# Windowed attention and a softplus feed-forward on one core: the holds on the first loads, and the order of the opening

## The chip, the cores and the metric

One core of one Trainium2 chip runs the whole program. The metric is the device time of one launch in microseconds (us); the runs of the kernel before had a median of 815.86 us (three runs, 813.49 to 820.68).

## The reference

```python
def _attn_ref(q, k, v):                    # 8 batches, 8 heads, 576 positions, 64 wide
    scores = scale * np.matmul(q, k.transpose(0, 1, 3, 2))
    mask_plain = (rel >= 0) & (rel < window)                                # window 32
    mask_dil = (rel >= 0) & (rel < window * dilation) & (rel % dilation == 0)   # dilation 4
    ...
    scores = np.where(masks[None, :, :, :], scores, -1000000000.0)
    attn = np.exp(scores - np.max(scores, axis=-1, keepdims=True))
    attn = attn / (np.sum(attn, axis=-1, keepdims=True) + 1e-09)
    return np.matmul(attn, v).astype(np.float32)

def _moe_ref(x, w_in, w_out):              # 4608 tokens, 512 wide, 2048 inside
    h = x @ w_in
    g = np.maximum(h, 0.0) + np.log1p(np.exp(-np.abs(h)))
    return (g @ w_out).astype(np.float32)
```

Half of the heads see the last 32 positions, half see 32 positions four apart. The result of the attention goes through a feed-forward layer with softplus between its two matrices. Inputs are float32; the two matrices come to the chip as 64-bit words.

## The kernel before

The 4608 tokens are nine chunks of 512. Four groups of two heads (two plain, two dilated) make a chunk's attention; their results, turned, are the chunk's x, and 16 slices of 128 columns of the inner layer follow. Each float32 operand of the large products is split into a high and a low part, so that a product is three matmuls. Later chunks go through a planner; both kernels share it and everything it makes.

The opening is not planned. It covers the first two chunks and the decoding of the first matrices, and its order is a string of words, OPENING (line 93). A loop behind the functions (from line 794 on) runs the words one by one. Each engine, and SP's queue of DMAs too, keeps the order in which the words issue its instructions. The words, with a group g, a chunk or a slice behind the letters:

- k, q, v, m, r: loads of a group's keys, queries and values, of a chunk's mask, and of a 128x512 piece of a matrix in 64-bit words (`raw`, two halves). All go to SP's queue except k0, k1 (line 758, on ACT's queue) and m0 (ACT's too).
- S: the scores of a group on TensorE, tile `s_ps`. For the first two chunks the mask is added by two more matmuls. M: the maximum (DVE, lines 410 and 415). E: eight exponentials (ACT, line 433). Z and P or Pv: sums, reciprocal, division (DVE, lines 445 to 453). T: four transposes on TensorE, tile `t_ps`. C or Cv: copying them out. V: the weighted values, tile `a_ps`. Xh, Xl: the high and low part of x.
- D0 to D5 and Dl: the seven steps that turn one `raw` piece into a matrix's high and low part, tile `parts`. D0 and D5 stand on ACT (lines 205 and 228), the others on DVE (207 to 231).
- H, A, G, Gs or Gh, Gl, O: the first product, softplus on ACT and DVE, its two parts `gh` and `gl` (line 704), the second product.
- F with a number: so many matmuls on a block of zeros that nobody reads, tile `unread` ("fillers").
- A word with @ behind it: its first load is held back until the last matmul of the word named there.

Besides the hold, `load_dma` (line 163) keeps at most eight of SP's first loads under way, and a load into a buffer waits for the last reader of what stood there. Queries of the first chunk have buffers of their own; q4, q5 and q6 use three in turn, and q7 takes that of q4. Every load raises one of eight semaphores, DMAHW0 to DMAHW7, taken in turn in the order in which the scheduler places the loads, and waits until the load that had that semaphore before it has landed.

```python
    def load_dma(engine=None, **kw):
        ins = tc.keep_in_program_order((engine or nc.sync).dma_start(**kw))
        if held[0] is not None:
            tc.add_manual_dep(
                ins.ins,
                held[0].ins.name,
    ...
    for word in OPENING.split():
        word, _, awaited = word.partition("@")
        held[0] = last_of.get(awaited)
    ...
        parts[name](*(int(x) for x in word[len(name) :].split("_")))
        last_of[word] = last_matmul[0]
```

Of the kernel before, what the change touches and what calls it, by code (L numbers as in the profile page):

```python
# [90 lines left out]


OPENING = """
k0 F1 m0 k1 q0 q1@F1 S0 M0 S1 E0 F6 r0 M1 Z0 r1 k2@S0 F1 q2 Pv0 D0_0_0 D0_1_0 E1 D1_0_0 q3 D1_1_0 S2 D2_0_0
D2_1_0 D3_0_0 v0 T0 M2 Z1 k3@S0 S3 m1@F6 r2@S1 C0 D3_1_0 Pv1 V0 D4_0_0 k4@S2 q4@F1 v1@F1 E2 D0_0_1 M3 k5@S3
D4_1_0 T1 Xh0 D5_0_0 S4 Cv1 r3@F1 q5@F1 D1_0_1 Z2 D2_0_1 Xl0 M4 E3 v2@F6 F3 Pv2 E4 V1 Xh1 Z3 T2 D0_2_0 Dl0_0
D3_0_1 Pv3 H0_0 Cv2 v3@V1 D5_1_0 S5 r4@S3 Xl1 D4_0_1 M5 T3 D1_2_0 C3 Dl1_0 r5 D5_0_1 V2 D2_2_0 Xh2 H0_1 E5 v4@T3
Xl2 Z4 H1_0 Pv4 Dl0_1 V3 Xh3 D3_2_0 Xl3 D4_2_0 D0_3_0 r6 D1_3_0 D2_3_0 T4 H0_2 C4 Z5 r7@H0_1 H0_3 H1_1 D0_1_1
D1_1_1 D5_2_0 A0 V4 v5@T4 D3_3_0 Xh4 Dl2_0 G0 H1_2 q7@H1_1 H1_3 Xl4 D0_4_0 Pv5 Gs0 H2_0 A1 r8@H0_2 D4_3_0 Gl0
H2_1 H2_2 k7@H0_3 T5 D1_4_0 D5_3_0 D2_1_1 H2_3 G1 k6@H2_2 O0_0 C5 Dl3_0 V5 D3_1_1 D2_4_0 O0_1 Gs1 Xh5 D0_2_1 r9  # L100
D4_1_1 O0_3 H3_0 H3_1 Gl1 Xl5 D1_2_1 D5_1_1 A2 D3_4_0 D2_2_1 Dl1_1 D4_4_0 S7 O0_2 G2 D0_5_0 H3_2 O1_1 M7 O1_2
D5_4_0 Dl4_0 H3_3 D3_2_1 r10 H4_0 Gs2 D1_5_0 r11 q6@O0_2 O1_3 E7 D4_2_1 v7@O0_2 D5_2_1 A3 H4_1 H4_2 Gl2 v6
D2_5_0 D0_3_1 D3_5_0 Dl2_1 D4_5_0 S6 M6 H4_3 D5_5_0 O2_1 O2_3 O2_2 O1_0 E6 D0_4_1 G3 Dl5_0 Z7 H5_0 D1_3_1 Pv7
D2_3_1 Z6 O2_0 r12 T7 H5_1 Gs3 D3_3_1 H5_2 C7 D4_3_1 D5_3_1 Gl3 D1_4_1 V7 Dl3_1 H5_3 D0_5_1 Xh7 D2_4_1 Pv6 Xl7
A4 D3_4_1 O3_0 O3_1 D1_5_1 r13@O2_1 r14@T7 T6 Cv6 D2_5_1 G4 O3_2 D4_4_1 O3_3 V6 A5 Xh6 D0_6_0 H6_0 r15 G5 Xl6
H6_1 H7_0 D3_5_1 H6_2 D5_4_1 H7_1 D4_5_1 D5_5_1 H7_2 Gh4 D0_6_1 Dl4_1 Gl4 H6_3 H7_3 Dl5_1 Gs5 r16 D1_6_1 A6
D2_6_1 r17@H6_1 D1_6_0 Gl5 O4_3 D0_9_0 O4_2 O4_0 O5_2 O4_1 O5_3 G6 D1_9_0 H8_0 O5_1 D2_9_0 D2_6_0 O5_0 H8_1 A7
H8_2 G7 Gh6 K0@O5_1 K1 H9_0 Gl6 r18@H8_0 r19 H8_3 D3_6_0 D3_6_1 K2 H9_1 O6_0 H9_2 D4_6_0 r20 K3 D3_9_0 O6_1 r21
O6_3 r22@O6_0 H9_3 D4_9_0 D4_6_1 r23@H9_3 Gs7 A8 Gl7 O7_3 O6_2 O7_2 O7_0 D5_9_0 D5_6_1 G8 r24 r25@O7_2 D5_6_0
Dl6_1 A9 r26 r27@H9_3 Dl6_0 Dl9_0 Gh8 Gl8 G9 O7_1 Gh9 Gl9 r28@O7_0 r29@O6_2 r30@O7_1 r31  # L110
"""


# [1542 lines left out]
```

## Time and profile before

| what | us |
|---|---|
| median of the runs | 815.86 |
| the profiled execution | 819.88 |
| its span, first to last instruction | 818.1 |
| TensorE busy in the span | 801.9 |
| DVE busy | 660.2 |
| ACT busy | 501.8 |

A row of the timeline or the chain gives the start, the duration and the instruction; what stands in brackets is the time that the engine was idle before, and what ended it. PE is TensorE, PEld its weight loads, SPq and ACTq are the queues on which DMAs are issued. A table by stages gives the length of a stretch, then for each engine the busy time and in brackets the number of instructions, then TensorE's granted clock as a share of the full one, the busy share of the DMA engines and what they moved.

### The profile page before, as it was taken

What the parts mean: (1) busy time and instruction counts of PE and PEld (TensorE: products, weight loads), DVE (VectorE), ACT (ScalarE), POOL (GpSimd) and SP (SyncE); (2) the same over time, 40 slices, a digit from 0 to 9 for tenths busy, and PEclk for the clock granted to TensorE, in tenths of its full rate; (3) what the DMA queues carried; (4) which work ended last, traced back from release to release, by engine and by line L of the source; (5) the groups of instructions that cost most, each with busy time, mean ns of one, the idle gap of its engine ahead of it and who ended that gap; (6) DMA issues with size and microseconds to landing.
All of it is one profiled execution on the core that took longest, in us unless ns stands there. A gap on an engine that the chain in (4) does not pass through costs nothing.

```text
span 818.1 us, 19668 instructions
## 1 busy us (share of the span) xinstructions
PE 801.9 (98%) x7833; PEld 654.2 (80%) x7835; DVE 660.2 (81%) x967; ACT 501.8 (61%) x1122; POOL 189.4 (23%) x132
## 2 busy tenths in 40 slices
PE   6999999999999999999999999999999999999998
PEld 4678888788888888888787888888888888888886
DVE  4798899957687766897999887897997846778974
ACT  5787788745666645596786413889943616775410
POOL 0000000054043324754313202202024302221510
PEclk9699999999999999999999999999999999999999
DMA  9774999968879673999988999879989675556573
GB/s 298 242 242 129 307 374 339 314 208 287 278 249 296 210 219 142 374 336 357 350 295 303 316 352 333 289 240 346 298 269 308 233 248 189 196 190 199 189 218 140
DMA packets 118490, 218.94 MB, mean 268 GB/s; under 512 B 11520, under 2 KB 53632, under 8 KB 118400
## 3 DMA queue, kind: packets, MB, share of 16 engines
q1 hardware_dynamic: 117968, 216.97, 79.1%
q8 instruction: 62, 1.02, 0.5%
q10 hardware_dynamic: 432, 0.72, 0.3%
q14 instruction: 28, 0.23, 0.1%
HBM read 162.07 MB, written 55.57 MB: 266 GB/s over the span
## 4 chain that ended last, share of the span: by engine, by line
PE 72%; DVE 10%; DMA 9%; ACT 5%; issue 2%; POOL 1%; SPq 0%; POOLq 0%; DVEq 0%; ACTq 0%
PE y L237 20%; PE z L237 12%; PE x L237 12%; PE h_ps L237 11%; PE o_ps L237 10%; PE a_ps L237 3%; DMA raw<-w 3%; PE s_ps L237 3%; DMA w_t<-cast 2%; ACT s L433 2%; ACT e L1308 1%; DVE g_of L940 1%; DVE a L216 1%; DMA v<-vp 1%; DMA k<-kdl 1%
## 5 line engine op out<-in xcount | busy, mean ns | idle before, releaser
L940 POOL TENSOR_TENSOR g_of<-g_of 128x1024 f32<-128x1024 f32 x33 | 80.3, 2434 | 258.6 <-DVE g_of L1311 133.3
L940 DVE TENSOR_TENSOR g<-g_of,g 128x1024 fp32r<-128x1024 f32 x84 | 121.3, 1450 | 15.0 <-ACT g L972 14.5
L237 PE MATMUL o_ps<-gh,parts 128*128 128x512 f32 x384 | 129.2, 394 | 0.0
L237 PE MATMUL h_ps<-xh,parts 128*128 128x512 f32 x384 | 129.1, 394 | 0.0
L972 ACT CAST g<-g_of 128x1024 fp32r<-128x1024 f32 x61 | 63.9, 1051 | 102.8 <-PE z L237 44.3
L1308 ACT ACTIVATE e<-e 128x1024 f32<-128x1024 f32 x96 | 101.1, 1058 | 1.7
L237 PE MATMUL y<-g,ring 128*128 128x512 f32 x432 | 100.5, 390 | 0.0
L237 PEld LDWEIGHTS y<-g,ring 128*128 128x128 f32 x432 | 80.8, 188 | 17.1
L940 POOL TENSOR_TENSOR b<-parts 128x512 f32<-128x512 f32 x29 | 40.4, 1393 | 213.5 <-DVE parts L231 143.8
L237 PEld LDWEIGHTS h_ps<-xh,parts 128*128 128x128 f32 x384 | 72.4, 188 | 15.6 <-DVE x_full L587 0.4
L237 PEld LDWEIGHTS o_ps<-gh,parts 128*128 128x128 f32 x384 | 72.1, 188 | 15.9
L433 ACT ACTIVATE s<-s,nm 128x64 f32<-128x64 f32 x224 | 74.8, 336 | 7.2 <-DVE nm L424 7.1
L237 PE MATMUL h_ps<-xl,parts 128*128 128x512 f32 x192 | 75.0, 391 | 0.0
L237 PE MATMUL o_ps<-gl,parts 128*128 128x512 f32 x192 | 74.8, 390 | 0.0
L237 PE MATMUL z<-g,ring 128*128 128x512 f32 x288 | 66.7, 390 | 0.5 <-DVE g L940 0.5
L237 PE MATMUL x<-g,ring 128*128 128x512 f32 x288 | 66.5, 390 | 0.0
L237 PE MATMUL z<-s_h,ring 128*128 128x512 f32 x192 | 63.3, 390 | 0.7 <-DVE temp L940 0.7
L237 PE MATMUL y<-s_h,ring 128*128 128x512 f32 x192 | 63.6, 392 | 0.3 <-DVE temp L940 0.3
L237 PEld LDWEIGHTS z<-g,ring 128*128 128x128 f32 x288 | 53.9, 188 | 12.1 <-DVE g L940 0.9
L237 PE MATMUL x<-a_h,ring 128*128 128x512 f32 x192 | 63.3, 390 | 0.0
L237 PEld LDWEIGHTS x<-g,ring 128*128 128x128 f32 x288 | 53.9, 188 | 11.5 <-DVE g L940 0.2
L940 DVE TENSOR_TENSOR g_of<-y,temp 128x512 f32<-128x512 f32 x60 | 39.6, 682 | 28.7 <-PE y L237 28.6
(111 smaller groups left out, 1522.4 us busy)
## 6 DMA issues: line engine op xcount, KB each, us to landing
ring<-w_t SPq DMA_DIRECT2D x96, 512.0 KB, 4.7
ring<-w_b SPq DMA_DIRECT2D x72, 512.0 KB, 5.1
raw<-w SPq DMA_DIRECT2D x64, 256.0 KB, 5.6
w_t<-cast SPq DMA_DIRECT2D x64, 256.0 KB, 5.5
w_b<-parts SPq DMA_DIRECT2D x48, 256.0 KB, 5.1
v<-vp SPq DMA_DIRECT2D x14, 512.0 KB, 5.7
x_full<-vp SPq DMA_DIRECT2D x14, 512.0 KB, 5.8
turned<-sq SPq DMA_DIRECT2D x112, 64.0 KB, 3.2
```

The lines of the kernel that those rows point to most:

```text
L216: pin(nc.vector.scalar_tensor_tensor(out=ai, in0=low, scalar=29, in1=ai, op0=ALU.logical_shift_right, op1=ALU.bitwise_or,))
L237: last_matmul[0] = tc.keep_in_program_order(nc.tensor.matmul(**kw))
L433: pin(nc.scalar.activation(out=self.blocks[:, t], in_=src, func=AF.Exp, bias=self.nm[:, t : t + 1], scale=1.0 / 8.0 if self.masked else 1. ...
L940: pin((nc.gpsimd if name == "POOL" else nc.vector).tensor_tensor(out=dst, in0=a, in1=b, op=op))
L972: pin(nc.scalar.copy(out=dst, in_=src))
L1308: pin(nc.scalar.activation(out=to(), in_=of(), func=func, **kw))
```

## The change

The string OPENING is replaced. No word of the new one has an @ behind it, so no load of the opening is held until a matmul. The words stand in another order, with the same loads, decode steps and products; k1 stands behind E0, r0 in front of all. The fillers are F1, F6, F1 and F3, where they were F1, F6, F1 and F3 at other places. The F01 of the new string is F1. The string is one line shorter, so line numbers are smaller by one. Its first lines:

```diff
 OPENING = """
-k0 F1 m0 k1 q0 q1@F1 S0 M0 S1 E0 F6 r0 M1 Z0 r1 k2@S0 F1 q2 Pv0 D0_0_0 D0_1_0 E1 D1_0_0 q3 D1_1_0 S2 D2_0_0
-D2_1_0 D3_0_0 v0 T0 M2 Z1 k3@S0 S3 m1@F6 r2@S1 C0 D3_1_0 Pv1 V0 D4_0_0 k4@S2 q4@F1 v1@F1 E2 D0_0_1 M3 k5@S3
...
+r0 q0 k0 m0 D0_0_0 D1_0_0 q1 S0 D2_0_0 D3_0_0 D4_0_0 r1 q2 k2 M0 r2 D5_0_0 E0 k1 D0_1_0 S1 F1 S2 M1 Dl0_0 Z0
+D1_1_0 Pv0 q3 v0 D0_0_1 D2_1_0 M2 D1_0_1 E1 k3 F6 D3_1_0 T0 q4 D2_0_1 D4_1_0 Z1 D3_0_1 F01 C0 S3 V0 E2 Xh0 Pv1
...
+v3 Xl1 D2_2_0 Dl1_0 Dl0_1 q7 T3 r4 V2 E4 H0_1 r5 Xh2 C3 D0_1_1 D0_3_0 D3_2_0 Xl2 D4_2_0 S5 M5 D1_3_0 D5_2_0 V3
...
```

ACT at the very start, before the change, with the semaphores that each waits for (k_79 is k0, k_85 is k1, raw_182 and raw_193 are r0 and r1):

```order
L164 DMA k_79<-kpl 128x544
L164 DMA opened_76<-cst 128x640
L164 DMA k_85<-kpl 128x544
L433 ACTIVATE s_126,sm_166<-s_ps_91,nm_127 128x64 [waits DVE_50,PE_50]
L433 ACTIVATE s_126,sm_166<-s_ps_91,nm_127 128x64 x7
L205 ACTIVATE a_203<-raw_182 128x512 [waits DMAHW6_50,DMAHW5_50]
L205 ACTIVATE a_205<-raw_193 128x512 [waits DMAHW7_50,DMAHW0_50]
```

The same engine at the same place now (k_84 is k0, k_156 is k1, raw_79, raw_131 and raw_142 are r0, r1 and r2):

```order
L163 DMA k_84<-kpl 128x544
L163 DMA opened_76<-cst 128x640
L204 ACTIVATE a_88<-raw_79 128x512 [waits DMAHW2_50,DMAHW1_50]
L227 CAST parts_145<-a_88 128x512 [waits DVE_50,Activation_50]
L432 ACTIVATE s_138,sm_147<-s_ps_93,nm_139 128x64 [waits DVE_50,PE_50]
L432 ACTIVATE s_138,sm_147<-s_ps_93,nm_139 128x64 x7
L163 DMA k_156<-kpl 128x544 [waits DMAHW4_50]
L204 ACTIVATE a_158<-raw_131 128x512 [waits DMAHW7_50,DMAHW6_50]
L204 ACTIVATE a_249<-raw_142 128x512 [waits DMAHW3_50,DMAHW2_50]
```

k1 moved from the third place to behind D0_0_0, D5_0_0 and E0. It waits for DMAHW4 until two loads have landed on it; these are q0 and q3, and S1 waits for k1 as the third.

SP's queue, from its start to the load of k3 now (q_82 to q_244 are q0 to q3, k_136 and k_266 are k2 and k3; before, q1, k2, m1 and k4 each waited for PE_50, a matmul):

```order
L163 DMA raw_79<-w 128x256 x2
L163 DMA q_82<-qp 128x512
L163 DMA q_91<-qp 128x512
L163 DMA raw_131<-w 128x256 x2
L163 DMA q_134<-qp 128x512 [waits DMAHW0_50]
L163 DMA k_136<-kdl 128x640 [waits DMAHW1_50]
L163 DMA raw_142<-w 128x256 [waits DMAHW2_50]
L163 DMA raw_142<-w 128x256 [waits DMAHW3_50]
L163 DMA q_244<-qp 128x512 [waits DMAHW4_50]
L163 DMA v_246<-vp 128x512 [waits DMAHW5_50]
L163 DMA v_246<-vp 128x512 [waits DMAHW6_50]
L163 DMA k_266<-kdl 128x640 [waits DMAHW7_50]
```

None of these waits for TensorE; each waits for an earlier load. q3 (q_244) moved ahead of k1 on DMAHW4, where q0 stands before it.

SP's queue a little further on, now (v_521 is v3, q_529 is q7, raw_537 and raw_586 are r4 and r5):

```order
L163 DMA v_521<-vp 128x512 [waits DMAHW4_50]
L163 DMA v_521<-vp 128x512 [waits DMAHW5_50]
L163 DMA q_529<-qp 128x512 [waits DMAHW6_50,PE_50]
L163 DMA raw_537<-w 128x256 [waits DMAHW7_50]
L163 DMA raw_537<-w 128x256 [waits DMAHW0_50]
L163 DMA raw_586<-w 128x256 [waits DMAHW1_50]
L163 DMA raw_586<-w 128x256 [waits DMAHW2_50]
```

q7, which stood behind r7 and v5 in SP's queue before, now stands between v3 and r4, and it waits for TensorE because of its buffer.

## Rows read from the trace of the kernel before

**Rows 1.** The page, part 1: busy us, share of the span, instructions.

```profile
PE 801.9 (98%) x7833; PEld 654.2 (80%) x7835; DVE 660.2 (81%) x967; ACT 501.8 (61%) x1122; POOL 189.4 (23%) x132
```

**Rows 2.** Table by stages, the engines' busy time in three stretches.

```profile
6.90:45.70 38.80, 34.17 (x719) 25.01 (x722) 29.46 (x73) 30.19 (x128) 0.00 (x0) 0.78 0.83 275
...
45.70:156.00 110.30, 109.08 (x1024) 89.02 (x1022) 104.47 (x202) 86.99 (x209) 1.42 (x1) 1.00 0.85 283
...
160.00:818.00 658.00, 652.51 (x5888) 535.62 (x5886) 521.84 (x687) 379.40 (x774) 186.93 (x125) 1.00 0.79 264
```

**Rows 3.** The chain that ended last, up to 50 us: start, us, what.

```profile
0.76 3.75 DMA k<-kpl
...
8.58 7.23 DMA k<-kdl
...
20.93 0.93 issue
...
45.78 0.69 PE o_ps L237 x3
```

**Rows 4.** Timeline of TensorE, 6 to 25 us: S1, fillers, S3, V0, T1, V1.

```profile
6.93 1.19 PE L237 MATMUL s_ps<-k,q 64*32 64x64 f32 x64 [0.66 <-DMA q<-qp]
...
9.30 2.56 PE L237 MATMUL unread<-opened 128*128 128x512 bf16 x5 [0.22 <-issue]
...
15.95 1.18 PE L237 MATMUL s_ps<-k,q 64*32 64x64 f32 x64 [1.87 <-DMA k<-kdl]
...
17.60 1.93 PE L237 MATMUL a_ps<-pt,v 64*64 64x32 f32 x64
19.47 1.11 PE L464 MATMUL t_ps<-opened,s 128*128 128x128 f32 x4
...
24.76 1.92 PE L237 MATMUL a_ps<-pt,v 64*64 64x32 f32 x61
```

**Rows 5.** Table by stages, the two stretches in which TensorE is slow.

```profile
16.40:33.70 17.30, 15.74 (x392) 11.83 (x373) 11.61 (x29) 10.25 (x48) 0.00 (x0) 0.51 0.70 235
...
4.50:11.90 7.40, 6.37 (x138) 3.21 (x139) 3.71 (x11) 4.26 (x23) 0.29 (x1) 1.00 0.96 315
```

**Rows 6.** Timeline of ACT, of ACT's and SP's queues: issues, and ACT's last raw.

```profile
1.66 0.45 ACTq L164 DMA_DIRECT2D k<-kpl  x1
2.33 2.53 SPq L164 DMA_DIRECT2D raw<-w  x4
...
6.31 0.33 SPq L164 DMA_DIRECT2D k<-kdl  x1
...
10.67 0.68 ACT L205 ACTIVATE a<-raw 128x512 f32<-128x512 f32 x1 [0.33 <-DMA raw<-w]
...
19.50 8.85 SPq L164 DMA_DIRECT2D v<-vp  x4
```

**Rows 7.** DMA in each us from 0 to 40, and a stretch.

```profile
GB/s 0 37 257 352 329 295 320 336 264 205 406 398 397 402 363 302 189 358 396 370 251 339 289 379 133 0 0 0 135 318 143 299 318 295 168 309 406 375 381 293
...
24.40:28.40 4.00, 3.59 (x71) 3.03 (x70) 2.72 (x7) 3.59 (x20) 0.00 (x0) 0.50 0.04 13
```

**Rows 8.** DMA issues to 40 us: KB each, median us to landing.

```profile
k<-kpl ACTq DMA_DIRECT2D x2, 272.0 KB, 4.6
```

**Rows 9.** Timeline of TensorE from 39 us, full clock: V, T, scores.

```profile
39.75 1.14 PE L237 MATMUL a_ps<-pt,v 64*64 64x32 f32 x64
...
44.48 0.60 PE L464 MATMUL t_ps<-opened,s 128*128 128x128 f32 x4
...
50.41 0.86 PE L237 MATMUL s_ps<-k,q 64*32 64x64 f32 x64
```

**Rows 10.** From DVE's second maximum to gl0: table by stages, and gl0 itself.

```profile
8.48:44.65 36.17, 31.57 (x648) 22.84 (x649) 28.13 (x69) 27.98 (x120) 0.00 (x0) 0.76 0.83 276
...
43.97 0.68 DVE L704 TENSOR_TENSOR gl<-e,gh 128x512 fp32r<-128x512 f32 x1
```

**Rows 11.** TensorE's waits from 36 us on: us, times, longest.

```profile
PE a_ps L237 <- DVE a L207: 1.4, 1, 1.4
```

More of the change, by code (lines that the diff above doesn't have):

```diff
@@ L93 @@
 OPENING = """
-k0 F1 m0 k1 q0 q1@F1 S0 M0 S1 E0 F6 r0 M1 Z0 r1 k2@S0 F1 q2 Pv0 D0_0_0 D0_1_0 E1 D1_0_0 q3 D1_1_0 S2 D2_0_0
-D2_1_0 D3_0_0 v0 T0 M2 Z1 k3@S0 S3 m1@F6 r2@S1 C0 D3_1_0 Pv1 V0 D4_0_0 k4@S2 q4@F1 v1@F1 E2 D0_0_1 M3 k5@S3
-D4_1_0 T1 Xh0 D5_0_0 S4 Cv1 r3@F1 q5@F1 D1_0_1 Z2 D2_0_1 Xl0 M4 E3 v2@F6 F3 Pv2 E4 V1 Xh1 Z3 T2 D0_2_0 Dl0_0
-D3_0_1 Pv3 H0_0 Cv2 v3@V1 D5_1_0 S5 r4@S3 Xl1 D4_0_1 M5 T3 D1_2_0 C3 Dl1_0 r5 D5_0_1 V2 D2_2_0 Xh2 H0_1 E5 v4@T3
-Xl2 Z4 H1_0 Pv4 Dl0_1 V3 Xh3 D3_2_0 Xl3 D4_2_0 D0_3_0 r6 D1_3_0 D2_3_0 T4 H0_2 C4 Z5 r7@H0_1 H0_3 H1_1 D0_1_1
@@ L99 @@
[L99 to L108, printed above, removed]
@@ L109 @@
-O6_3 r22@O6_0 H9_3 D4_9_0 D4_6_1 r23@H9_3 Gs7 A8 Gl7 O7_3 O6_2 O7_2 O7_0 D5_9_0 D5_6_1 G8 r24 r25@O7_2 D5_6_0
-Dl6_1 A9 r26 r27@H9_3 Dl6_0 Dl9_0 Gh8 Gl8 G9 O7_1 Gh9 Gl9 r28@O7_0 r29@O6_2 r30@O7_1 r31
+r0 q0 k0 m0 D0_0_0 D1_0_0 q1 S0 D2_0_0 D3_0_0 D4_0_0 r1 q2 k2 M0 r2 D5_0_0 E0 k1 D0_1_0 S1 F1 S2 M1 Dl0_0 Z0
+D1_1_0 Pv0 q3 v0 D0_0_1 D2_1_0 M2 D1_0_1 E1 k3 F6 D3_1_0 T0 q4 D2_0_1 D4_1_0 Z1 D3_0_1 F01 C0 S3 V0 E2 Xh0 Pv1
+T1 M3 v1 D4_0_1 Cv1 m1 k4 S4 Xl0 E3 r3 Z2 D0_2_0 V1 v2 D5_1_0 Pv2 T2 M4 q5 Xh1 Z3 D5_0_1 k5 H0_0 D1_2_0 Pv3 Cv2
@@ new lines @@
+v3 Xl1 D2_2_0 Dl1_0 Dl0_1 q7 T3 r4 V2 E4 H0_1 r5 Xh2 C3 D0_1_1 D0_3_0 D3_2_0 Xl2 D4_2_0 S5 M5 D1_3_0 D5_2_0 V3
+Z4 D2_3_0 H0_2 F3 H1_0 Xh3 Xl3 H0_3 Dl2_0 Pv4 H1_1 r6 E5 r7 T4 H1_2 D1_1_1 r8 v4 r9 H1_3 A0 Z5 D2_1_1 D3_3_0 Pv5
+C4 D0_4_0 v5 k7 V4 G0 H2_0 v6 Gs0 D4_3_0 r10 H2_1 Xh4 k6 r11 D1_4_0 Gl0 Xl4 H2_2 D3_1_1 T5 A1 D4_1_1 O0_3 O0_0
+C5 D2_4_0 V5 H2_3 D5_1_1 q6 r12 r13 D3_4_0 Dl1_1 D5_3_0 D4_4_0 O0_1 D0_2_1 Xh5 D0_5_0 O0_2 Dl3_0 G1 Gs1 Xl5
+D5_4_0 A2 D1_2_1 H3_0 S7 Gl1 H3_1 H3_2 D2_2_1 v7 D1_5_0 O1_3 H3_3 M7 D2_5_0 E7 O1_2 O1_1 D3_2_1 r14 G2 D4_2_1
@@ new lines @@
+D5_2_1 r15 Gs2 D3_5_0 Dl4_0 O1_0 S6 Z7 Gl2 A3 H4_0 Dl2_1 M6 D4_5_0 D0_3_1 H4_1 H4_2 O2_1 H4_3 G3 O2_0 D5_5_0
+D1_3_1 Dl5_0 Pv7 E6 D2_3_1 O2_2 H5_0 D3_3_1 r16 T7 H5_1 D0_4_1 O2_3 Z6 H5_2 C7 Pv6 Gs3 D4_3_1 D1_4_1 r17 V7
+D5_3_1 Dl3_1 Gl3 D2_4_1 H5_3 O3_3 O3_2 A4 Xh7 D3_4_1 Xl7 O3_0 G4 D4_4_1 T6 O3_1 H6_0 r18 D0_5_1 Cv6 Gh4 r19 A5
+V6 D5_4_1 r20 H6_1 G5 H7_0 Dl4_1 Gl4 Gs5 D1_5_1 Xh6 D0_6_0 Xl6 D2_5_1 O4_0 D0_9_0 D3_5_1 D1_9_0 D4_5_1 D5_5_1
+D1_6_0 O4_1 H6_2 Dl5_1 O4_2 H6_3 H7_1 H7_2 Gl5 D2_6_0 O4_3 r21 H7_3 A6 D0_6_1 O5_0 G6 D3_6_0 Gh6 D4_6_0 D2_9_0
@@ L111 @@
+A7 O5_1 D1_6_1 K0 O5_2 H8_0 O5_3 D5_6_0 H8_1 K1 D3_9_0 K2 G7 Gl6 D4_9_0 Gs7 Dl6_0 K3 H9_0 D2_6_1 D5_9_0 H9_1
+H8_2 r22 D3_6_1 r23 H8_3 r24 Gl7 H9_2 r25 A8 D4_6_1 H9_3 O6_3 O6_0 Dl9_0 A9 O6_1 O6_2 D5_6_1 O7_3 O7_1 O7_2 r26
+G8 O7_0 G9 Gh8 r27 r28 Dl6_1 Gl8 Gh9 r29 r30 Gl9 r31
 """
```

## The prediction

> **What bounds the kernel now.** I read the table by engine first: TensorE is busy 801.9 us of a span of 818.1 [rows 1], so only 16.2 us of waiting and whatever the clock costs can move. The table by stages says where these lie [rows 2]. From 6.9 to 45.7 us TensorE works 34.17 of 38.80, from 45.7 to 156 it works 109.08 of 110.30, and 5.5 us of waiting lie behind 160 us, where the instructions of both kernels stand in the same order on every engine. So the change is decided before 45.7 us, where the first product of the second matrix begins, and what it costs or brings there is handed on: behind it TensorE has almost no gap into which a delay could fall.
>
> The chain of waits shows what the opening waits for [rows 3]: k0 for 3.75 us, the scores S0, then k3, issued at 8.58 and 7.23 us under way, then S3 at 15.95 and from there TensorE's own work, with 0.93 us of "issue" at 20.93, up to the first O at 45.78. The timeline of TensorE adds that S1 began at 6.93, that fillers stood behind it, and that S3 waited 1.87 us for k3 [rows 4]. The clock is the other loss. [...] The record says 1.00 from 4.5 to 11.9, but scores take as long there as in the slow stretch (S1 1.19, S3 1.18 without their masks), and five fillers take 2.56, so I count TensorE slow up to about 11.9 as well.
>
> **The change part by part.** The holds on a matmul go: SP's queue no longer waits for TensorE at k2 (issued 6.31), at m1, k4 and k5, or at v3, where the four halves of v2 and v3 take SP from 19.50 to 28.35 and the 16 DMA engines are 4% busy from 24.4 to 28.4 [rows 6, 7]. But the new words also move one load behind two waits. k1, issued on ACT at 1.66 before [rows 6], now stands on ACT behind the first decode step, the cast D5_0_0 and E0, and it waits for the semaphore DMAHW4 to come round. On that semaphore lie q0, then q3, then k1, and k1's wait is for two landings. So k1 is issued when q3 has landed, and S1, the second step of TensorE, waits for k1. Everything behind S1 on TensorE is late with it: S2, T0, S3, V0.
>
> When does q3 land? Up to and with q3 the two queues hold 3312 KB, 3.39 MB. In the kernel before, 2240 KB (2.29 MB) had landed at 10.67, when ACT got the last half of raw, and 3904 KB (4.00 MB) at 15.9, with k3 [rows 4, 6]. That is 1.71 MB in 5.2 us, 0.33 MB per us, and gives 14.0 for q3. Without the hold of 1.45 us at k2 (last raw issued by 4.86, k2 at 6.31) and at the 406 GB/s that the DMA engines moved at 10 us [rows 7] it is 10.67 - 1.45 + 1.10/0.406 = 11.9. I take 13.4, nearer to the first, since the queue behind is as deep in both. k1 itself: the two k on ACT's queue took 4.6 us [rows 8], k0 alone 3.75, k3 behind SP's full queue 7.23 [rows 3]. I take 4.6, the row of the same transfer on the same queue. **S1 then begins at 13.4 + 0.1 + 4.6 = 18.1**, between 15.7 (11.9 + 3.75) and 21.3 (14.0 + 7.23), where it began at 6.93.
>
> [...]
>
> From S1 on I add TensorE's work in the new order, at the slow clock, which it surely has: it will have been idle from about 8.7 to 18, and 1.87 us were enough for the fall at 16. S1 1.74, one filler 0.43, S2 1.72, six fillers 2.6, T0 1.04, a filler 0.43: S3 begins at 18.1 + 7.96 = 26.1, 10.1 us late. Then S3 1.72, V0 1.9, T1 1.04 and S4 1.7: V1 begins at 32.5, where it was at 24.76 [rows 4]. So 2.4 us come back there: three fillers (0.43 each) that the new words put behind V3, their gap, and the 0.93 us of issue. From V1 on the order is nearly the old one, and **at the slow clock the delay stays +7.7 us**.
>
> What takes some of it back is the clock. Before, TensorE worked slowly for 7.4 us at the start (4.5 to 11.9) and for 17.3 us in the long stretch, 15.74 of them busy, before the clock rose [rows 5]. In the new order it works without a gap from 18.1, so the rise falls between 25.5 and 35.4. The same work slow and fast: scores 1.18 and 0.86 without their masks, V 1.93 and 1.14, T 1.11 and 0.60 [rows 4, 9]. If the rise is at 25.5, V0 and V1 save 0.8 each, T1 and T2 0.5 each, S3 and S4 some 0.5 each with their masks: 3.6 us, and +4.1 remains at T2's end.
>
> The other engines set a floor. DVE's step M1 waits for S1, and up to gl0, which the second product of the first O reads, 65 of its instructions follow in the new order; before, 68 lay between 8.48 and 44.65, busy 28.13 us [rows 10]. 28.13 x 65/68 = 26.9 from 19.9 (S1 plus its 1.74) ends at 46.8, **+2.1 us** even if DVE never waits. It does wait, for scores and transposes. ACT had 27.98 us busy in the same stretch and is delayed by the same S1.
>
> A second wait that the title does not tell: q7 now stands in SP's queue ahead of r4, and its buffer is that of q4, so it waits for S4 on TensorE. S4 is over at about 32.5, so r4 to r8 are issued from there on; r4 was issued right behind v3 before, at 28.4 [rows 6]. The decoding that feeds the H parts is late by some 4 us too, which the cover of the late TensorE hides; if TensorE is not late it costs up to these 4 us.
>
> I take +5.0 at 45.7 us, about the middle between DVE's +2.1 and the slow clock's +7.7. Fillers are 11 for 11. The 1.40 us at 156 that TensorE waits for DVE [rows 11] could swallow at most 1.4 if DVE is less late than TensorE; I take nothing. **Sum: 819.88 + 5.0 = 824.9 for the profiled execution.** That one lies 4.0 us above the median of the runs, 815.86, and I put the change on the median: **821**. Bounds: -0.3 - 1.4 with S1 at 15.7 and DVE's floor, 814; and with S1 at 21.3 and the slow clock +10.9, 827.
>
> **The rivals.**
> *The early loads pay.* [...] As a mechanism here: k1 lands at 15.7, TensorE works without a gap from there, the clock rises at 23.1 and stays. S3 begins at 23.7 and V1, by the savings above, at 27.8, 3.0 late; V1 and T2 save 1.3, and the work up to 33.7, which was slow before, some 3 us more by the same ratios. TensorE would be 1.3 us early, DVE's floor allows 0.3 (44.4 for 44.65), and the 1.40 at 156 goes: 814. Against it: every price has to lie at its low end. 0.18.
>
> *The delay is hidden.* S1 is late, but DVE and ACT have done r0's decoding by then (DVE's first four steps now stand ahead of M0), the floor holds and the wait at 156 gives 1.4 back: +2.1 - 1.4, 816.6. For it speaks that DVE is 104.5 of 110.3 us busy up to 156 [rows 2], so it is DVE that ends last there. Against it: TensorE has the same instructions to do and no idle time to do them in. 0.12.
>
> *The holds come back as buffers and semaphores, slower by over 1%.* SP is stopped at q7 until S4, ACT at k1 until q3, and k1 takes 7.23: S1 at 21.3, S4 done near 35.7, r4 issued 7 us later than before, and the clock stays at half until after 35. 7.7 + 3.2 = +10.9, 827. It decides where S1 begins after 18.5 and the clock stays low through V1 (7.7 + 0.4 is the 1%). For it: the DMA engines are full from 3 us on, at about 300 GB/s [rows 7]. 0.22.
>
> **How the numbers follow.** The forecast (818 to 824) has 0.48, the rivals 0.18, 0.12 and 0.22. About 1% is what a measurement of this kernel can tell from no change: its three runs lie between 813.5 and 820.7. Slower by over 1% is above 824.0: the last rival and an edge of the forecast, 0.25. Faster by over 1% is below 807.7, beyond DVE's floor; I keep 0.06 for a floor that I counted wrongly. Within 1%: 0.69. The range goes from the first rival less the spread of the runs, 812, to the last one plus a little, 828.
>
> **What would show it.** In the new profile: k1's issue on ACT at 12 to 14 us, S1 at 16 to 21 with TensorE idle from 9, DVE's M1 right behind it, no waits of SP for TensorE before q7, then one that ends with S4, and the first O at 48 to 53. If S1 begins before 14, the reading of the semaphore is wrong; if the first O comes before 44, DVE's floor is; if the clock is full before 23, the first rival gains.

## The result, and the profile after

The change makes the kernel slower. Six runs of each have medians of 829.1 us (824.69 to 830.28) after and 817.0 us (813.49 to 820.74) before, a ratio of 1.0138 with a 95% interval of 1.0112 to 1.0163. The profiled execution of after took 829.36 us, 9.48 more than that of before (819.88).

Page, part 1, of after (busy us, share of the span, instructions), against [rows 1]:

```profile
PE 797.4 (96%) x7835; PEld 651.7 (79%) x7835; DVE 660.0 (80%) x967; ACT 501.7 (61%) x1122; POOL 189.9 (23%) x132
```

TensorE is busy 4.5 us less than before in a span that is 9.4 us longer (827.5 for 818.1). It worked faster on average, and waited 14 us more. The table by stages says where. The stretches are those of [rows 2], the last two moved by the 9.36 us by which the first O is late (54.98 us, where it was 45.62):

```profile
6.90:55.06 48.16, 31.38 (x785) 22.96 (x785) 30.43 (x74) 29.67 (x126) 0.29 (x1) 0.93 0.70 241
55.06:165.36 110.30, 110.30 (x1080) 90.16 (x1081) 102.96 (x200) 86.82 (x205) 1.42 (x1) 1.00 0.87 296
169.36:827.36 658.00, 651.72 (x5885) 535.16 (x5883) 522.68 (x688) 379.99 (x775) 187.50 (x125) 1.00 0.78 263
```

Behind the first O nothing is lost: no wait at all up to 165 us, and some 0.8 us more waiting in the long rest. All of it is lost before the first O. TensorE's waits up to 62 us name three large ones (us, times, longest):

```profile
PE s_ps L236 <- DMA k<-kpl: 8.9, 1, 8.9
PE s_ps L236 <- DMA q<-qp: 7.7, 1, 7.7
PE s_ps L236 <- issue: 4.2, 1, 4.2
PE t_ps L463 <- DVE s L452: 1.0, 1, 1.0
```

The first is S1's wait for k1, which the prediction is about. The second is S0's for q0 (S0 began at 4.56 before), which now stands behind r0 on SP's queue. The third has no semaphore behind it. The timeline of TensorE shows the three places, with S0, S1 and S2, a row of fillers, V0, T2, V2, the first matmul of H0_1, the two pieces of S5, V3, the fillers F3, T5 and the first O:

```profile
7.70 1.17 PE L236 MATMUL s_ps<-k,q 64*32 64x64 f32 x64 [7.70 <-DMA q<-qp]
...
18.36 1.18 PE L236 MATMUL s_ps<-k,q 64*32 64x64 f32 x64 [8.94 <-DMA k<-kpl]
...
20.44 1.09 PE L236 MATMUL s_ps<-k,q 64*32 64x64 f32 x64
...
21.69 1.46 PE L236 MATMUL unread<-opened 128*128 128x512 bf16 x6
...
25.20 1.13 PE L236 MATMUL a_ps<-pt,v 64*64 64x32 f32 x64
...
31.96 0.63 PE L463 MATMUL t_ps<-opened,s 128*128 128x128 f32 x4 [0.79 <-DVE sm L444]
...
34.19 1.20 PE L236 MATMUL a_ps<-pt,v 64*64 64x32 f32 x64
...
35.32 0.50 PE L236 MATMUL h_ps<-xh,parts 128*128 128x512 f32 x1
...
36.21 0.72 PE L236 MATMUL s_ps<-k,q 64*32 64x64 f32 x48
41.09 0.35 PE L236 MATMUL s_ps<-k,q 64*32 64x64 f32 x16 [4.15 <-issue]
...
41.69 1.89 PE L236 MATMUL a_ps<-pt,v 64*64 64x32 f32 x64
...
44.96 1.50 PE L236 MATMUL unread<-opened 128*128 128x512 bf16 x3
...
54.63 0.60 PE L463 MATMUL t_ps<-opened,s 128*128 128x128 f32 x4
54.98 0.48 PE L236 MATMUL o_ps<-gh,parts 128*128 128x512 f32 x1
```

Of the same places before, T2, the first matmul of H0_1 and the first O (T5 is the row at 44.48 in [rows 9]):

```profile
27.45 1.11 PE L464 MATMUL t_ps<-opened,s 128*128 128x128 f32 x4
...
33.88 0.50 PE L237 MATMUL h_ps<-xh,parts 128*128 128x512 f32 x1
...
45.62 0.40 PE L237 MATMUL o_ps<-gh,parts 128*128 128x512 f32 x1
```

S5 stops behind its 48th matmul for 4.15 us, in the middle of equal instructions on tiles that are long there. The durations tell the clock as well: S1 is slow (1.18), S2 still takes 1.09, the six fillers and V0 are fast (1.46 for six, 1.13, against 2.56 for five and 1.93 in [rows 4]), and after the stop V3 and the fillers are slow again (1.89, and 1.50 for three). So the clock had risen by 21.7, some three microseconds after S1 began. The table by stages of after says the same of the clock from there on (sixth value behind the length of the stretch); ahead of that it reads 1.00 even where S1 is slow (18.3 to 19.6 us), so there only the durations count:

```profile
20.40:36.90 16.50, 13.61 (x468) 10.05 (x468) 16.19 (x43) 14.53 (x76) 0.00 (x0) 1.00 0.57 183
...
41.00:48.70 7.70, 7.61 (x94) 5.50 (x94) 5.93 (x16) 3.03 (x18) 0.00 (x0) 0.56 0.63 239
```

**Where the 9.36 us come from.** H0_1 begins at 35.32, where it began at 33.88: +1.44 (the delay of 11.4 us of S1 had shrunk that far). From H0_1 to the first O before took 11.74 us and after takes 19.66. Of the 7.9 more, 4.15 are the stop in S5. The slow clock behind it costs some 3.1: the 184 matmuls from the end of the stop to the first O take 13.89 us here, and 10.77 in the run with k1 early and r4 held until T2 below, where the clock is full and nothing waits for long. S5 itself (0.72 and 0.60, up to V3) and F3 (0.82 at full clock) now stand behind H0_1 and stood in front of it; that is 2.1 of work that only changed sides. H2_3 changed sides the other way: before it stood in front of the first O (0.8 us), now it stands behind. And 0.5 us of waiting for ACT, which before had there, is gone. Together that is 8.1, near enough to the 7.9. At T5, behind the same work in both, the delay is 10.15 (54.63 for 44.48): 4.15 and 3.1 are the stop and its clock, 7.3 together, and the late start costs the rest, some 3 us.

### The profile page after: what moved, and what is told of

The parts are those of the page before. It is cut to its first block, busy times and chain, and to the rows that moved or that the text cites. A ratio compares the mean times of both kernels' runs of the same rounds, so it can differ in the third digit from the quotient of the medians.

```text
span 827.5 us, 19651 instructions
## 1 busy us (share of the span) xinstructions
PE 797.4 (96%) x7835; PEld 651.7 (79%) x7835; DVE 660.0 (80%) x967; ACT 501.7 (61%) x1122; POOL 189.9 (23%) x132
## 4 chain that ended last, share of the span: by engine, by line
PE 84%; DMA 6%; DVE 5%; issue 2%; ACT 1%; SPq 1%; POOL 1%; POOLq 0%; ACTq 0%; DVEq 0%
PE y L236 23%; PE x L236 14%; PE z L236 14%; PE o_ps L236 14%; PE h_ps L236 14%; PE a_ps L236 3%; PE s_ps L236 3%; DMA ring<-w_t 2%; DMA raw<-w 1%; DVE g_of L939 1%; DMA w_t<-cast 1%; DVE g L939 1%; DMA x_full<-rows 1%; DMA out_t<-ob 1%; DVE g_of L1310 1%
## 5 line engine op out<-in xcount | busy, mean ns | idle before, releaser
L236 PE MATMUL h_ps<-xh,parts 128*128 128x512 f32 x384 | 131.0, 397 | 0.0
L236 PEld LDWEIGHTS x<-g,ring 128*128 128x128 f32 x288 | 53.9, 188 | 11.4
L939 DVE TENSOR_TENSOR g_of<-y,temp 128x512 f32<-128x512 f32 x60 | 39.7, 684 | 28.7 <-PE y L236 28.6
```

Of the source, the lines that this page charges most:

```text
L236: last_matmul[0] = tc.keep_in_program_order(nc.tensor.matmul(**kw))
L939: pin((nc.gpsimd if name == "POOL" else nc.vector).tensor_tensor(out=dst, in0=a, in1=b, op=op))
```

## Experiments

Two theories were on the table. One is the prediction's: k1 comes late, and all is late with it. The other: TensorE stood for want of instructions, and this, not data, is what the opening runs into. A rival to the second was chance, or a data wait that the trace doesn't name. Ratios are to the kernel before, run beside each kernel on the same chip, with 95% intervals.

### The change again

No edit. 

> The changed kernel once more, unaltered. Theory A (the 4.15 us without a semaphore in the middle of S5, and the half clock behind it, belong to this order of the words): the stall stands again at the same matmul of S5, 3 to 5 us long, the first O of the second product begins at 54 to 56 us, and the ratio to the kernel before is 1.011 to 1.016. Rival B (a chance event of the one profiled execution): no idle time of more than 1 us in S5, the first O near 47 to 49 us in this profile, and the profiled execution some 7 us shorter than 829.

829.5 us, ratio 1.0118 (1.0094 to 1.0142). TensorE stops at the same matmul for 3.60 us, and the first O begins at 54.21. The stop belongs to the kernel.

### The holds alone

All @ of the old words are taken away and nothing is moved:

```diff
-k0 F1 m0 k1 q0 q1@F1 S0 M0 S1 E0 F6 r0 M1 Z0 r1 k2@S0 F1 q2 Pv0 ...
+k0 F1 m0 k1 q0 q1 S0 M0 S1 E0 F6 r0 M1 Z0 r1 k2 F1 q2 Pv0 ...
```

> The kernel before with every @ of its words taken away and nothing moved: the holds alone. If the holds themselves were worth something (theory A: loads that come too early fill the DMA engines ahead of k3 or of TensorE's instructions), it is slower than before by 1 to 6 us, with S3 later than 15.95 or an idle time of TensorE without a semaphore before 45 us. Rival B (the holds cost, and the loss of the change lies in the new order alone): S3 and V0 as before, the hole of the DMA engines at 24 to 28 us gone, first O at 43 to 45.5 us, 0 to 3 us faster.

818.0 us, ratio 0.9995 (0.9975 to 1.0014): the holds alone are worth nothing in either direction. The timeline of TensorE in this run shows why (S3, V0, the two pieces of S4, the two of V1, the first O):

```profile
16.19 0.93 PE L236 MATMUL s_ps<-k,q 64*32 64x64 f32 x64 [1.16 <-DMA k<-kdl]
...
17.37 1.14 PE L236 MATMUL a_ps<-pt,v 64*64 64x32 f32 x64
...
20.73 0.83 PE L236 MATMUL s_ps<-k,q 64*32 64x64 f32 x61 [1.32 <-issue]
...
22.46 1.12 PE L236 MATMUL a_ps<-pt,v 64*64 64x32 f32 x61
26.92 0.42 PE L236 MATMUL a_ps<-pt,v 64*64 64x32 f32 x3 [3.33 <-issue]
...
45.06 0.40 PE L236 MATMUL o_ps<-gh,parts 128*128 128x512 f32 x1
```

The clock is full where before it was slow (V0 1.14 for 1.93 in [rows 4]), and the DMA engines have no hole at 24 to 28 us any more (341 GB/s on average in the first 40 us, 270 before). What that brings is given back in two stops without a semaphore, 1.32 and 3.33 us. With the second the clock falls as well (0.65 on average from 27 to 35 us), and S1 waits 2.86 us for k1 and begins at 9.09, where it began at 6.93. Before had both stops too, shorter and at the same matmuls: 0.93 us [rows 3] and 0.41.

### k1 where it was

```diff
-r0 q0 k0 m0 D0_0_0 D1_0_0 q1 S0 ... D5_0_0 E0 k1 D0_1_0 S1 F1 ...
+r0 q0 k0 m0 k1 D0_0_0 D1_0_0 q1 S0 ... D5_0_0 E0 D0_1_0 S1 F1 ...
```

> The changed kernel with k1 issued right behind m0 on ACT, as before. Theory A (the late S1 itself was mostly made good by the earlier clock, 1.4 us were left at H0_1; the loss is the stall in S5 and the slow clock behind it): S1 begins at 7 to 10 us instead of 18.36, but if a stall of 3 to 4 us comes again at the same count of TensorE's instructions, the first O is still at 51 to 55 us, and the kernel is 0 to 4 us faster than the change. Rival B (k1's place is the whole loss, as the prediction had it): first O at 45 to 46.5 us, 8 to 10 us faster than the change, equal to the kernel before or better.

822.7 us, ratio 1.0047 (1.0030 to 1.0063): 6 to 7 us of the loss hang on k1's place, more than Theory A allowed. S1 begins at 9.52 and S5 at 30.86, 5.35 us earlier than in the change; TensorE stops for 1.47 us in S4 and for 2.78 us in S5, again behind its 48th matmul, and the first O begins at 46.75, 1.1 us behind that of before. Of the 8.23 us by which the first O is earlier than in the change, 5.35 are there when S5 begins, 1.37 are the shorter stop, and 1.5 are the work behind it, with less of it at the lower clock (12.38 for 13.89). So the truth lies between: the late S1 is the larger part of the loss, though not all of it, and the stop stays.

### q7 behind v5

```diff
-v3 Xl1 D2_2_0 Dl1_0 Dl0_1 q7 T3 r4 V2 ...
+v3 Xl1 D2_2_0 Dl1_0 Dl0_1 T3 r4 V2 ...
-C4 D0_4_0 v5 k7 V4 ...
+C4 D0_4_0 v5 q7 k7 V4 ...
```

> The changed kernel with q7 put behind v5, in front of k7, so that r4 to r9 need not wait behind it for S4. Theory A (the ten halves of raw that SP issues in one go from 29 us on, after q7's wait, stand in front of the block of instructions that TensorE needs in S5): without the burst the stall of 4.15 us shrinks under 1 us, the clock stays full, first O at 46 to 49 us, 5 to 8 us faster than the change. Rival B (the stall hangs on when TensorE reaches that count of instructions, not on the burst): the stall stays at 3 to 4 us at the same matmul, first O at 53 to 55 us, within 1.5 us of the change.

828.2 us, ratio 1.0122 (1.0083 to 1.0160), no difference from the change. S5 runs through, but now TensorE stops in three other places: 0.64 us in S3, 1.96 in S4 and 2.32 in T2, where V1 ends. SP issues raw from 19.86 on without a pause. The loads that were freed filled the DMA engines earlier (busy 0.97 of the first 28.6 us, 0.78 in the change), and the stops moved to where they were full. The first O begins at 52.05. Theory A is right that the stop leaves S5, and wrong that the time goes with it; the wait for q7 costs nothing that the median shows.

With k1 in its old place as well:

> The changed kernel with k1 behind m0 and q7 behind v5: what is left of the change is the other order of the words. Theory A (with k1 early TensorE is bound by its blocks of instructions, wherever the loads stand): stalls of 1 to 2 us in S3 to S4 and of 1.5 to 3.5 us in V1 or S5, first O at 44.5 to 47 us, ratio 0.998 to 1.005. Rival B (the rest of the loss with k1 early was q7's wait): first O before 44 us and faster than the kernel before by 2 us or more.

823.3 us, ratio 1.0061 (1.0034 to 1.0089): stops of 1.70, 2.42 and 2.71 us, a first O at 48.74 in a profiled execution that was 3 us above its median. Rival B falls; the stops are as Theory A has them, the first O is later.

### Where the stops are

If TensorE gets its instructions in blocks, as I suppose, the place of a stop is a count, and moves when instructions are added in front:

```diff
-r0 q0 k0 m0 D0_0_0 D1_0_0 q1 S0 D2_0_0 ...
+r0 q0 k0 m0 D0_0_0 D1_0_0 q1 S0 F16 D2_0_0 ...
```

> The changed kernel with 16 more fillers (a weight load and a matmul each) behind S0, where TensorE is idle for 9 us anyway. [...] Rival B (S5 waits at a place of its own, for data or a buffer that the trace does not name): the stall stays behind S5's 48th matmul.

830.5 us, ratio 1.0138 (1.0087 to 1.0189). The timeline of TensorE in this run, V0, V1 and S5 in two pieces each:

```profile
26.14 1.02 PE L236 MATMUL a_ps<-pt,v 64*64 64x32 f32 x56
28.42 0.32 PE L236 MATMUL a_ps<-pt,v 64*64 64x32 f32 x8 [1.26 <-issue]
...
30.49 1.26 PE L236 MATMUL a_ps<-pt,v 64*64 64x32 f32 x48
32.52 0.43 PE L236 MATMUL a_ps<-pt,v 64*64 64x32 f32 x16 [0.77 <-issue]
...
37.03 0.46 PE L236 MATMUL s_ps<-k,q 64*32 64x64 f32 x32
41.58 0.68 PE L236 MATMUL s_ps<-k,q 64*32 64x64 f32 x32 [4.09 <-issue]
```

The stop in S5 moved from the 48th matmul to the 32nd, 16 forward, for 16 fillers. So its place is a count, and rival B falls. The stops of over 0.4 us in the openings of all these runs stand behind 220, 345 to 347, 472 to 474 and 598 to 600 matmuls, with as many weight loads: one place every 253 or so instructions. The table by stages counts them (matmuls, then weight loads, in the brackets), here for the kernel before up to its 0.93 us of issue, and for after up to the stop in S5:

```profile
0.00:20.93 20.93, 13.77 (x346) 8.54 (x347) 9.63 (x25) 12.42 (x59) 1.02 (x6) 0.89 0.91 296
```

```profile
0.00:37.00 37.00, 17.41 (x600) 12.37 (x601) 19.80 (x51) 20.87 (x97) 1.02 (x6) 1.00 0.78 263
```

The page of after (part 3: packets, MB, share) has a queue for it:

```profile
q8 instruction: 62, 1.02, 0.5%
```

That is 16 KB a packet, and 62 packets for TensorE's 15,670 matmuls and weight loads make one for 253. Such a packet comes before every stop ends: of the 26 stops of over 0.4 us in the openings of the 17 traces, 25 end 2.2 to 2.6 us after a packet of this queue starts, and one 3.4 us after. TensorE's other waits of that length from 12 us on end anywhere from 0 to 8.9 us after one. The DMA part of the page of after for two short stretches, from 32 to 38.6 us without one and the next 0.2 us with one; TensorE goes on at 41.09, 2.4 us behind it:

```profile
q1 hardware_dynamic: 1019, 1.86, 94.5%
q14 instruction: 1, 0.01, 0.5%
...
q1 hardware_dynamic: 31, 0.06, 98.7%
q8 instruction: 1, 0.02, 30.0%
```

### Fewer loads under way

The number of SP's first loads that may be under way is halved. In the change:

```diff
-DEPTH = 8
+DEPTH = 4
```

> The changed kernel with at most 4 instead of 8 of SP's first loads under way. [...] Rival B (the block's delay does not depend on what is under way): stall still 3.5 us or more. Rival C (four loads of 256 KB are too few to keep the DMA engines busy): the DMA engines move under 300 GB/s in the first 20 us, and S1 begins after 20 us.

825.7 us, ratio 1.0095 (1.0068 to 1.0122), by the ratios 2 to 3.5 us faster than the change, with intervals that overlap. The stop in S5 is gone and one of 2.98 us stands in S4, where the change had none: the loads that were over by 24 us in the change (25 GB/s and less from 24 to 29 us) now run on to 30 us (162 to 363 GB/s from 24 to 29). k1 took 5.14 us for 5.32; S1 begins at 15.91, as k1 is issued earlier. No theory is decided.

The old words without holds, and the new ones with k1 early, also with DEPTH 4:

> The kernel before without any hold, with at most 4 loads under way. Without holds and with 8 under way the clock was full from 13 us, but stalls of 1.32 and 3.33 us at 19.4 and 23.6 gave it back. Theory A: the two stalls fall to under 2 us together, the clock stays at its full level past 30 us, S3 within 1 us of 16.2, first O at 40 to 43.5 us, 2 to 5 us faster than the kernel before. Rival C (too few loads under way): r4 to r7 land later, first O at 45 us or behind, 0 to 4 us slower.

829.5 us, ratio 1.0141 (1.0084 to 1.0198), though the first O at 45.69 is as early as before. S4 waits 3.06 us for q4, V1 runs through, V2 stops for 2.05 us. The loss lies behind the first O, where TensorE waits 5.0 us for a load and 3.3 us for DVE once each. Rival C, and more of it than it had: the DMA engines moved 253 GB/s in the first 40 us, for 341 with eight under way.

> The changed kernel with k1 behind m0 and at most 4 loads under way. With 8 under way the stalls were 1.47 us at 21.9 and 2.78 us in S5, the first O at 46.75. Theory A: the stalls together fall from 4.3 to under 2 us, first O at 43.5 to 45.5 us, 1 to 3 us faster than with 8 under way, and the ratio to the kernel before 0.998 to 1.003. Rival B: stalls unchanged, 822 to 824 us.

827.7 us, ratio 1.0103 (1.0048 to 1.0157). There are no stops at all, and S3 waits 3.52 us for k3, the clock falls (V0 takes 1.94 us for 1.13 in the change), and the first O comes at 49.74. Here Theory A is right on the stops and wrong on the time: fewer loads under way traded one wait for another.

### The loads behind the block

To see whether the loads make the block late, r4 and what stands behind it on SP's queue are held back until TensorE has got it:

```diff
-v3 Xl1 D2_2_0 Dl1_0 Dl0_1 q7 T3 r4 V2 E4 ...
+v3 Xl1 D2_2_0 Dl1_0 Dl0_1 q7 T3 r4@T3 V2 E4 ...
```

> The changed kernel with one hold put back: r4 waits for T3, so that the ten halves of raw are issued from about 34.2 us on and not from 29.2, and nothing is under way when TensorE begins the block of instructions that ends in S5, at about 31 us. Theory A (that block's successor was late only because it landed behind the loads issued at 29 to 35 us): no stall, or one under 1 us, in S5, the clock stays full, S5 done by 38 us; then DVE and ACT lack raw for some us, first O at 48 to 52 us, 2 to 6 us faster than the change. Rival B (the delay of a block hangs on something else): stall of 3 us or more in S5 again and, with raw 5 us later, 2 to 5 us slower than the change.

827.3 us, ratio 1.0106 (1.0076 to 1.0137). The stop is 1.96 us, between the two forecasts. From 31 to 34 us the DMA engines moved next to nothing (27, 0 and 8 GB/s in the three us), and the block still came only at 35.6, when r4, issued from 33.01 on, was already running. Why it did not come in the empty stretch no run shows. So that r4 is not under way at 35 us either, the hold goes behind V2:

```diff
-v3 Xl1 D2_2_0 Dl1_0 Dl0_1 q7 T3 r4 V2 E4 ...
+v3 Xl1 D2_2_0 Dl1_0 Dl0_1 q7 T3 V2 r4@V2 E4 ...
```

> The changed kernel with r4 held until V2 instead of T3. [...] Theory A (the delay is the loads in front of the block): with r4 starting behind 35.5 us the block comes by 35.5 and the stall in S5 is 0.2 to 1.0 us (4.15 in the change, 1.96 with the hold at T3). Theory B (half of the delay is a way of its own that no load order shortens): 1.7 to 2.2 us again. In both, r4 to r8 are 6 us later than in the change, so the time is 825 to 830.

825.4 us, ratio 1.0097 (1.0064 to 1.0130). The timeline of TensorE, T3, V2, the two pieces of S5, a wait for ACT, and the first O:

```profile
33.73 0.66 PE L463 MATMUL t_ps<-opened,s 128*128 128x128 f32 x4 [0.33 <-DVE pt L501]
34.31 1.20 PE L236 MATMUL a_ps<-pt,v 64*64 64x32 f32 x64
...
36.33 0.72 PE L236 MATMUL s_ps<-k,q 64*32 64x64 f32 x48
37.37 0.35 PE L236 MATMUL s_ps<-k,q 64*32 64x64 f32 x16 [0.31 <-issue]
...
43.27 0.49 PE L236 MATMUL h_ps<-xh,parts 128*128 128x512 f32 x1 [1.91 <-ACT xh L615]
...
51.97 0.47 PE L236 MATMUL o_ps<-gh,parts 128*128 128x512 f32 x1
```

V2 begins within 0.12 us of where it does in the change (34.19), so what differs from there to the stop in S5 is the loads alone. The DMA part of the page of this run for 32 to 34.7 us, and for the 0.2 us behind it:

```profile
q14 instruction: 1, 0.01, 0.8%
...
q8 instruction: 1, 0.02, 33.3%
```

The block comes 3.9 us earlier, and the stop is 0.31 us instead of 4.15. And the clock stays up; the table by stages of this run from the end of the stop to the first O, and of the change for the same 184 matmuls:

```profile
37.37:51.97 14.60, 11.69 (x184) 8.31 (x184) 10.20 (x24) 10.38 (x31) 0.00 (x0) 1.00 0.99 321
```

```profile
41.09:54.98 13.89, 13.89 (x184) 10.51 (x184) 9.93 (x23) 8.80 (x28) 0.00 (x0) 0.75 0.43 152
```

(The 14.60 us have 2.9 of waiting in them.) Theory A is confirmed: the block was late because of the loads in front of it. Three delays of the loads give three stops: 4.15 us in the change, 1.96 with the hold at T3, 0.31 here. The clock fell with the first two (V3 behind the stop took 1.89 and 1.93 us) and stayed up with the third (1.00 in the table). The first O is 3.0 us earlier than in the change, not 6, since the raw that was held is missed: TensorE waits 1.91 us for x's high part, which stands on ACT behind a raw that has not landed.

The block is on a queue of its own (q8) and still came 3.9 us later behind q1's loads (38.6 for 34.7).

The same hold with k1 early, first until T2:

> [...] Theory A: the stall in S5 falls under 0.7 us, that of 1.4 us in S4 stays, first O at 43.5 to 45.5 us instead of 46.75, ratio to the kernel before 0.998 to 1.003. Rival B: stall of 2 us or more in S5 and r4 late as well, first O at 47 to 50 us.

822.0 us, ratio 1.0029 (1.0005 to 1.0053); S5 stops for 1.01 us (2.78 with k1 early alone), S4 for 1.37 (1.47 there), and the first O begins at 44.82. This is the best of the versions with the new words. The table by stages from the end of the stop in S5 to the first O, the same 184 matmuls as above:

```profile
34.05:44.82 10.77, 10.70 (x184) 8.36 (x184) 9.80 (x23) 8.96 (x29) 0.00 (x0) 1.00 0.69 254
```

Then until V2:

> k1 behind m0 and r4 held until V2. With k1 early alone the stall in S5 was 2.78 us, with the hold at T2 1.01. Theory A: 0 to 0.5 us in S5, the 1.4 us in S4 stay, first O at 44 to 45.5 us, ratio 0.998 to 1.003. Theory B: 0.8 to 1.5 us again, and r4 3 us later than with the hold at T2: first O behind 45.5, ratio 1.002 to 1.007.

823.3 us, ratio 1.0073 (1.0048 to 1.0098). S5 runs through, as Theory A says; but the raw is now so late that TensorE waits 4.25 us for ACT and the first O comes at 50.36. And without the fillers of that stretch:

```diff
-Z4 D2_3_0 H0_2 F3 H1_0 Xh3 ...
+Z4 D2_3_0 H0_2 H1_0 Xh3 ...
```

> The same without the three fillers F3 behind H0_2, where TensorE has work of its own to do: nothing but 0.7 to 1.3 us of TensorE's time goes, if TensorE sets the end there; first O 0.7 to 1.3 us earlier than in the run with them, ratio 0.997 to 1.002. If DVE or a late r4 sets the end: first O the same within 0.3 us.

822.5 us, ratio 1.0063 (1.0042 to 1.0083): the first O at 49.84, 0.5 us earlier, and TensorE's wait for ACT grows to 5.00 us. That lies between the two forecasts, and the pair does not say what the fillers cost: TensorE goes on 1.59 us earlier than with them (39.98 for 41.57), but then takes 9.86 us to the first O where it took 8.79, at a granted clock of 0.70 for 0.81.

### A hold for the old words

The old words without holds stopped for 1.32 us in S4, from 19.4 us on, and for 3.33 us in V1, from 23.6 on, the second time behind v2, v3 and r4 (the packet came at 24.4). One hold is put back, at another place than before:

```diff
-q5 D1_0_1 Z2 D2_0_1 Xl0 M4 E3 v2 F3 Pv2 E4 V1 ...
+q5 D1_0_1 Z2 D2_0_1 Xl0 M4 E3 v2@S4 F3 Pv2 E4 V1 ...
```

> The kernel before with all holds taken away but one, on v2, which now waits for S4 (22 us) where it waited for the six fillers. [...] Theory A: with v2, v3 and r4 out of the way that stall falls under 1.7 us; that of 1.3 us at 19.4 stays; the clock stays full beyond 27 us; first O at 43 to 44.5 us, 0.5 to 3 us faster than the kernel before. Rival B: the stall stays above 2.5 us and the loads are 3 us late: equal to the kernel before or up to 3 us slower.

818.7 us, ratio 0.9996 (0.9976 to 1.0016). V1 runs through and the first O begins at 43.04 in the profiled execution, 2.6 us earlier than before. But S4's stop grew to 1.87 us and the clock fell (0.63 from 16 to 30 us), and over ten runs nothing is left. The kernel before was not beaten by any version tried.

## Why the prediction was wrong

**k1: right.** "k1 is issued when q3 has landed", at 12 to 14 us, and S1 at 18.1. In the profile of the change k1 is issued at 13.00, and S1 begins at 18.36. In the second profile of the change k1's issue follows q3's landing (13.42); in the first it follows E0's last exponential (12.93), so the two waits end together. k1 took 5.32 us for the 4.6 taken; the two k of the same size on SP's queue took 5.0, so ACT's queue was not seen to be the quicker one. Undoing this one move brings back 6 to 7 of the 11 to 12 us of the medians. That is more than the 3 us of the late start: with it go 1.37 us of the stop and 1.5 behind it, and with k1 early the new words are even some 1.8 us ahead of the old ones at H0_1 (29.97 for 33.88, with the 2.1 of S5 and F3 still to do).

**q7: right, and of no consequence,** as the run with q7 behind v5 shows. SP waits 9.5 us for TensorE's scores there; without that wait the stops came elsewhere and the time stayed.

**The clock: wrong, on the side of the faster.** "The rise falls between 25.5 and 35.4." It had risen by 21.7, some three microseconds after S1 began, as the fillers and V0 show. That S1 would be slow was right (1.18); that 1.87 us of waiting are always enough for that the runs do not show, as 1.91 us with the hold at V2 left the clock at 1.00. The first rival named a full clock before 23 as its sign, and did not win all the same. The delay at T2's end was +4.0 (32.59 for 28.56), the +4.1 that the sum gave for a rise at 25.5; that was luck, since with the earlier rise TensorE waited 2.4 us ahead of T2 (0.99, 0.58 and 0.79), for DVE mostly. At H0_1 it was +1.44, and some +3 at equal work at T5 without the stop. The +5.0 taken for the late start was thus 2 us too high.

**"Issue": the step that failed.** I counted "the 0.93 us of issue" at 20.93 [rows 3] among what comes back in the new order. It is not a loss that an order removes. It is the mark of TensorE running out of instructions, behind 346 matmuls, as the counts and the packets of the experiments show. In S4 it did go; in S5, two blocks on, it came back as 4.15 us. The new order puts TensorE at full clock on scores and weighted values, 128 instructions in 0.86 us and in 1.14, while SP fills the DMA engines from 29 us on. TensorE is at the end of its block at 36.94, the next one comes at 38.6, and 4.15 us go; with that stop the clock falls and costs some 3.1 more. Neither is in the sum or in a rival. The 3 us of the late start and these 7.3 make the 10.15 at T5, and with H2_3 now behind it the 9.36 at the first O, where the prediction had 5.0.

**DVE's floor: right as a floor, and never reached.** It stood at 46.8, and the first O came at 54.98; DVE was busy only 5.93 us of the 7.70 behind the stop (the row from 41.00 above). **The 1.40 at 156** is gone, as the second rival said; it pays for H2_3 and the 0.8 us more of waiting behind 160 us, and the end (9.4) is as late as the first O.

**From the profiled execution to the median: wrong too.** The sum gave 824.9 for the profiled execution, and 4.0 us were taken off to get 821, because the profiled execution of before lies that far above the median of its three runs. That distance did not recur: after's profiled execution, 829.36, is 0.3 us above the median of 829.1. Before's median of six is 817.0, and beside the experiments it was 817.0 to 818.9, so the 815.86 was low. Of the 8.2 us from 820.9 to 829.1, 4.5 are missing in the sum and 3.7 are this step.

**The range** ended at 828 because its worst case was S1 at 21.3 and a clock that stays low, less the same 4.0 us; a stop for instructions had no price in it. The third rival, 827, came nearest in time, but neither of its own terms occurred: k1 in 7.23 us and a clock that stays low.

**Taking the holds away** is worth nothing on this kernel: with the holds gone and nothing else changed the ratio is 0.9995. Loads come earlier (341 GB/s in the first 40 us for 270), and TensorE's instructions come later (stops of 1.32 and 3.33 us for 0.93 and 0.41).

What is left open: what starts a block's packet. The runs say only that the one of the block that begins in S5 did not come while the DMA engines were empty around T2 and T3 (31.7 to 34 us), and came within half a microsecond of V2's start when they still were. Why the profiled gain of 2.6 us at the first O with v2 held until S4 does not show in the median was not tried.

## What to carry to other kernels

"Issue" in a chain of waits of TensorE is worth a count: here the stops stood at even distances, every 126 or so matmuls with as many weight loads, and TensorE was waiting for instructions. On this kernel they stood in small products (128 instructions in 0.86 us at full clock) or in front of them; between 55 and 165 us, where the large ones stand, there was no wait at all. Loads issued earlier than needed were then not free here, even where the DMA engines had a hole: behind ten halves of raw the next block of instructions came 3.9 us later (38.6 for 34.7). Before a hold is taken away, look at what else its pause lets through; and before a load is moved on a queue, at everything that its new place makes it wait for, which on this kernel was the larger part of the loss.

## What the runs showed of the hardware that was not expected

- Queue q8, "instruction", moved 62 packets of 16 KB, one for some 253 of TensorE's matmuls and weight loads, and after a stop TensorE went on some 2.2 to 2.7 us after such a packet started (38.6 and 41.09 in the change, 34.7 and 37.37 with the hold at V2, 24.4 and 26.92 without holds), once 3.4 (35.6 and 39.06 with the hold at T3).
- Such a packet came 3.9 us later behind loads on another queue, q1, where SP had issued ten halves of raw, 256 KB each, from 29.17 us on (38.6 in the change for 34.7 with the hold at V2).
- A stop of 4.15 us between equal matmuls was followed, less than a microsecond after TensorE went on, by a granted clock of 0.50; one of 0.31 us was not, nor a wait of 1.91 us in the same run (with the hold at V2), while the wait of 1.87 us in the kernel before was [rows 4, 5]. What decides between the last two the runs do not show.
- After 8.94 us without work TensorE was at full speed some 3 us after S1 began (six fillers in 1.46 us from 21.69 on), where before it stayed slow for 17.3 us, busy 15.74 of them [rows 5].
